# Joining the sign and the low bits of a 64-bit weight: a 16-bit write beside the sign, a shift with one source, and one joining operation

## The chip, the cores and the metric

The kernel runs on one core of a Trainium2 chip. The metric is device time in microseconds (us), lower is better; the runs of the kernel before have a median of 466.94 us. The engines are named as in the profile: PE is TensorE (matrix products), DVE is VectorE, ACT is ScalarE, POOL is GpSimd, SP is the engine that issues most transfers.

## The reference

A block-wise linear attention with decay runs over 2 x 8 heads, 768 positions and 64 dimensions in 12 blocks of 64. Its output, as 1536 tokens of 512 numbers, goes through two layers one after the other.

```python
for b in range(nb):                                   # 12 blocks of 64 positions
    intra = (qb @ kb.T * Dmask) @ vb
    inter = (qb * lam_pow) @ kv_state
    out[:, :, sl] = intra + inter
    kv_state = lam_block * kv_state + (kb * rev_pow).T @ vb
x = out as (1536, 512)
h = x @ moe_w_in;  g = maximum(0.01 * h, h);  x = g @ moe_w_out      # 512 -> 2048 -> 512
h = x @ moe2_w_in; solu = h * softmax(h)                             # 512 -> 1024
ln = (solu - mean) / sqrt(var + 1e-6) * moe2_g_ln
return ln @ moe2_w_out                                               # 1024 -> 512
```

The kernel receives the weight matrices as 64-bit words, read as pairs of 32-bit integers; the second word of a pair has the sign and the high part of the number, the first word the rest of it.

## The kernel before, in words

A weight tile `raww` holds 128 partitions x 2 halves x 512 pairs of words; `raw[:, :, 0]` is the low word, `raw[:, :, 1]` the high word of a pair (stride 8 bytes). Twenty-four tiles come in the list `order`: 16 of kind "io" (one half for `w_in`, one for `w_out`), 4 of kind "a", 4 of kind "b". Each is turned into a 32-bit number `x` by five operations and then split into a high and a low part for products in two terms:

- `words(n)` on ACT: L291 scales the high word, read as float32, into `x`; L292 scales the upper 16 bits of the low word into a small integer.
- `convert(n)` on DVE: L300 clamps `x`; L301 and L302 shift it by three bits and put in sign and low bits.
- `high(n)` on ACT (L322) rounds `x` to the high part in `wio`, `low(n)` on DVE (L340) subtracts to get the low part.

The first two tiles are converted in halves (IN, OUT: 512 columns), the others whole (1024 columns), so L300, L301 and L302 each occur 26 times: 4 times with 512 and 22 times with 1024 columns.

Every engine executes its instructions in the order in which the function writes them; nothing reorders them. The attention steps 0 to 3 are written out by hand at the start, mixed with the conversion of tiles 0 and 1. Step s has scores on PE (L169), their masking on DVE (`scores_ev`, L177), products L201, L210 and L183 on PE, the state update on DVE (L194), and the copies of x to `xhi` (ACT, L256) and `xlo` (DVE, L260); POOL scales with decays (`scale_k` L153, `scale_q` L141, `decay_state` L163). Then a loop runs over 48 items (block of 512 tokens, chunk of w_in): item i does 12 products L350 into one of two banks `hps`; ACT applies the leaky maximum in place (L353) and copies (L356); DVE subtracts (L357); then the high and low part of tile i+1, `convert` of i+2, `words` of i+3; and PE does the 12 products L366 of item i-1. Item 2 also does the scores of step 4 into the other bank, `spare`, between its L350 and its L366; L177 for them is written behind `high` and `low` of tile 3, and item 3's L350 write to that bank. Items 0 to 2 have their `convert` and `words` placed by hand:

```python
        if i == 1:
            words(3)
            convert(3)
            words(4)
        else:
            convert(pair_at(i, 2))
            words(pair_at(i, 3))
```

After the 48 items come twelve token tiles of the second layer (L384, the normalization, transposes L424, L446).

Of the kernel before, what the change touches and what calls it, by code (L numbers as in the profile page):

```python
# [11 lines left out]
U16 = mybir.dt.uint16  # L12
AF = mybir.ActivationFunctionType
ALU = mybir.AluOpType
# [23 lines left out]
LO_SCALE = 7.4375 / 2.0**16  # L38
# [3 lines left out]
def fused_kernel(ctx: ExitStack, tc: tile.TileContext, att, vt, tab, cst, w_in, w_out, w_in2, w_out2, out):  # L42
# [13 lines left out]
    pe, dve, act, pool, sync = nc.tensor, nc.vector, nc.scalar, nc.gpsimd, nc.sync  # L56
# [227 lines left out]
    def words(n, halves=BOTH):  # L284
        if n >= len(order):
            return
        raw = raws[n][:, halves].rearrange("p h a b -> p (h a) b")
        if n not in xs_t:
            xs_t[n] = tmp.tile([P, 2, 512], F32, tag="s", name="x")
        x = xs_t[n][:, halves].rearrange("p h a -> p (h a)")  # L290
        act.activation(x, raw[:, :, 1].bitcast(F32), AF.Copy, scale=HI_SCALE)  # L291
        act.activation(raw[:, :, 0], raw.bitcast(U16)[:, :, 1], AF.Copy, scale=LO_SCALE)  # L292

    def convert(n, halves=BOTH):
        if n >= len(order):
            return
        raw = raws[n][:, halves].rearrange("p h a b -> p (h a) b")
        x = xs_t[n][:, halves].rearrange("p h a -> p (h a)")
        xu = x.bitcast(U32)
        dve.tensor_scalar(x, x, HI_MAX, -HI_MAX, op0=ALU.min, op1=ALU.max)  # L300
        dve.scalar_tensor_tensor(raw[:, :, 0], xu, 3, raw[:, :, 0], op0=ALU.logical_shift_left, op1=ALU.bitwise_or)  # L301
        dve.scalar_tensor_tensor(xu, xu, 0x80000000, raw[:, :, 0], op0=ALU.bitwise_and, op1=ALU.bitwise_or)  # L302

    hi_t = {}

# [183 lines left out]
    x_early(0, xb[0])  # L489
    state_ev(0, kb)  # L490
    words(0, IN)
    x_hi(0, xb[0])
    words(0, OUT)
    convert(0, IN)
    x_lo(0, xb[0])
    decay_state(1, pool)
# [7 lines left out]
    state(1, kb)  # L504
    low(0, IN)
    convert(0, OUT)
    scale_k(2, act)
    x_hi(1, xb[1])
# [13 lines left out]
    scores_ev(3, sb)  # L522
    state_ev(2, kb)
    words(1, IN)
    x_hi(2, xb[0])
    x_lo(2, xb[0])
    convert(1, IN)
    words(1, OUT)
    x_early(3, xb[1])
# [157 lines left out]
```

## Time and profile before

| | |
|---|---|
| median of 3 runs | 466.94 us (466.72, 466.94, 468.98) |
| the profiled execution's own time | 467.06 us |
| its span | 465.3 us (time 1.76 us above the span) |
| mean granted TensorE clock | 0.989 of full speed |
| busy in the span | PE 449.8 us, DVE 262.1, ACT 187.2, POOL 53.3 |

The span runs from the first to the last instruction on the core; times in the views below count from its start. A group of matmuls shows when the first began and how long until the last ended, and the bracket behind a row gives the idle time of that engine before it, with the instruction that ended the wait.

### The profile page before, as it was taken

To read this page: it belongs to the slowest core of one execution; us is meant where nothing else is said; L and a number is where in the kernel's file an instruction comes from. 1 tells how busy PE (TensorE), PEld (TensorE's weight loads), DVE (VectorE), ACT (ScalarE), POOL (GpSimd) and SP (SyncE) were. 2 spreads that over 40 slices of the span, in tenths; PEclk is the share of its full clock that TensorE was granted. 3 is DMA by queue.
4 is the path that set the end of the run, shared out by engine and by line. 5 is a ranking of instruction groups with operands and counts; after the bars stand their busy time and mean duration, and the time that the engine had idled before them with its cause. 6 is when DMAs were issued, how large, how long until landed. Compare 5 with 4: busy or idle time off the path is not lost.

```text
span 465.3 us, 7890 instructions
## 1 busy us (share of the span) xinstructions
PE 449.8 (97%) x3332; PEld 370.8 (80%) x3332; DVE 262.1 (56%) x417; ACT 187.2 (40%) x311; POOL 53.3 (11%) x57
## 2 busy tenths in 40 slices
PE   6788999999999999999999999999999999999997
PEld 3765788888888888888888888888888888888886
DVE  4697899999832121211131888912877666666651
ACT  3657667557332222122244777622322222222221
POOL 2434041240403030100000000000000000000000
PEclk9798999999999999999999999999999999999999
DMA  8999064931302020100015542000000000000001
GB/s 273 337 350 370 4 229 173 323 118 66 92 0 93 1 92 1 46 0 2 1 48 213 191 180 92 0 0 2 0 24 23 24 23 23 24 23 24 23 24 45
DMA packets 16659, 41.61 MB, mean 89 GB/s; under 512 B 1904, under 2 KB 4976, under 8 KB 16112
## 3 DMA queue, kind: packets, MB, share of 16 engines
q1 hardware_dynamic: 16400, 40.71, 24.9%
q8 instruction: 26, 0.43, 0.4%
q10 hardware_dynamic: 224, 0.39, 0.3%
q14 instruction: 9, 0.07, 0.0%
HBM read 37.95 MB, written 3.15 MB: 88 GB/s over the span
## 4 chain that ended last, share of the span: by engine, by line
PE 90%; DMA 3%; DVE 3%; ACT 1%; issue 1%; SPq 0%; ACTq 0%
PE hps L350 28%; PE acc L366 27%; PE acc L446 14%; PE hps L384 7%; PE aps L384 7%; DMA ldw<-in_att_dram 3%; PE acc L424 2%; PE aps L210 2%; PE aps L201 2%; PE hps L169 1%; DVE raww L301 1%; DVE x L302 1%; ACT wio L322 0%; DVE xlo L260 0%; DVE state L194 0%
## 5 line engine op out<-in xcount | busy, mean ns | idle before, releaser
L350 PE MATMUL hps<-xhi,wio 128*128 128x512 f32 x384 | 104.0, 393 | 3.2 <-ACT wio L322 2.2
L357 DVE TENSOR_TENSOR glo<-hps,ghi 128x512 fp32r<-128x512 f32 x48 | 33.2, 691 | 122.5 <-ACT ghi L356 121.2
L366 PE MATMUL acc<-ghi,wio 128*128 128x512 f32 x384 | 96.0, 392 | 0.0
L350 PEld LDWEIGHTS hps<-xhi,wio 128*128 128x128 f32 x384 | 72.3, 189 | 19.2 <-ACT wio L322 2.6
L353 ACT ACTIVATE hps<-hps 128x512 f32<-128x512 f32 x48 | 28.0, 582 | 143.4 <-PE hps L350 143.4
L366 PEld LDWEIGHTS acc<-ghi,wio 128*128 128x128 f32 x384 | 71.4, 188 | 15.1
L350 PE MATMUL hps<-xlo,wio 128*128 128x512 f32 x192 | 52.3, 395 | 1.2 <-DVE xlo L260 1.2
L366 PE MATMUL acc<-glo,wio 128*128 128x512 f32 x192 | 51.3, 389 | 0.0
L446 PE MATMUL acc<-wb,lnhi 128*128 128x512 f32 (+1 forms) x208 | 46.0, 374 | 0.3 <-ACT lnhi L432 0.3
L350 PEld LDWEIGHTS hps<-xlo,wio 128*128 128x128 f32 x192 | 36.5, 191 | 9.4 <-DVE xlo L260 1.7
L446 PEld LDWEIGHTS acc<-wb,lnhi 128*128 128x128 f32 x208 | 36.9, 188 | 7.4 <-ACT lnhi L432 0.6
L366 PEld LDWEIGHTS acc<-glo,wio 128*128 128x128 f32 x192 | 36.1, 188 | 7.5
L416 POOL TENSOR_TENSOR small<-small,nhalf 128x1 f32<-128x1 f32 x12 | 6.6, 548 | 251.7 <-DVE small L415 243.3
L301 DVE SCALAR_TENSOR_TENSOR raww<-x,raww 128x1024 uint32<-128x1024 uint32 (+1 forms) x26 | 32.0, 1231 | 1.2 <-ACT raww L292 0.3
L302 DVE SCALAR_TENSOR_TENSOR x<-x,raww 128x1024 uint32<-128x1024 uint32 (+1 forms) x26 | 31.6, 1214 | 0.9
L291 ACT ACTIVATE x<-raww 128x1024 f32<-128x1024 f32 (+1 forms) x26 | 27.9, 1073 | 2.2 <-DMA raww<-in_w_in_dram 2.2
L356 ACT CAST ghi<-hps 128x512 fp32r<-128x512 f32 x48 | 28.2, 587 | 1.5
L292 ACT ACTIVATE raww<-raww 128x1024 uint32<-128x1024 uint16 (+1 forms) x26 | 28.0, 1077 | 0.0
L141 POOL TENSOR_TENSOR qk<-qk,qpow 128x512 f32<-128x512 f32 x8 | 12.2, 1525 | 122.5 <-PE hps L169 122.5
L384 PE MATMUL hps<-wa,xhi 128*128 128x512 f32 x96 | 24.2, 394 | 0.0
L384 PE MATMUL aps<-wa,xhi 128*128 128x512 f32 x96 | 24.2, 394 | 0.0
L446 PE MATMUL acc<-wb,lnlo 128*128 128x512 f32 (+1 forms) x104 | 24.0, 373 | 0.0
(82 smaller groups left out, 527.1 us busy)
## 6 DMA issues: line engine op xcount, KB each, us to landing
raww<-in_w_out_dram SPq DMA_DIRECT2D x24, 512.0 KB, 6.8
raww<-in_w_in_dram SPq DMA_DIRECT2D x16, 512.0 KB, 6.8
raww<-in_w_in_dram SPq DMA_DIRECT2D x4, 1024.0 KB, 4.8
out_dram<-osb SPq DMA_DIRECT2D x11, 256.0 KB, 2.0
qk<-in_att_dram SPq DMA_DIRECT2D x8, 256.0 KB, 4.2
qk<-in_att_dram SPq DMA_DIRECT2D x16, 128.0 KB, 4.6
kv<-in_att_dram SPq DMA_DIRECT2D x8, 256.0 KB, 3.0
kv<-in_vt_dram SPq DMA_DIRECT2D x8, 256.0 KB, 3.8
```

What stands on the lines that cost most here:

```text
L141: eng.tensor_tensor(qs_t[s], q, qpow, op=ALU.mult)
L291: act.activation(x, raw[:, :, 1].bitcast(F32), AF.Copy, scale=HI_SCALE)
L292: act.activation(raw[:, :, 0], raw.bitcast(U16)[:, :, 1], AF.Copy, scale=LO_SCALE)
L301: dve.scalar_tensor_tensor(raw[:, :, 0], xu, 3, raw[:, :, 0], op0=ALU.logical_shift_left, op1=ALU.bitwise_or)
L302: dve.scalar_tensor_tensor(xu, xu, 0x80000000, raw[:, :, 0], op0=ALU.bitwise_and, op1=ALU.bitwise_or)
L350: pe.matmul(bank, w[:, s, k], x[b][:, k], start=(i == 0), stop=(i == len(terms) - 1))
L353: act.activation(bank, bank, AF.Prelu, alpha=0.01)
L356: act.copy(ghi, bank)
L357: dve.tensor_tensor(glo, bank, ghi.bitcast(F32), op=ALU.subtract)
L366: pe.matmul(acc[m], w[:, s, m], g, start=(f == 0 and first), stop=(f == NF - 1 and last))
L384: pe.matmul(bank, x[b][:, k, o : o + P], w2_t["a", k, half][:, s], start=(i == 0), stop=(i == len(terms) - 1),)
L446: pe.matmul(po[:, 0:n], x[:, k], w2_t["b", k][:, s, cols], start=(i == 0), stop=(i == len(terms) - 1))
```

## The change

L292 writes its small integer (0 to 7) as a 16-bit integer into the lower half of the high word, beside the sign, where it went as a 32-bit integer into the low word. L301 now only shifts `x` in place: one source, one scalar (`tensor_scalar`), where it was an operation with two tensor sources that also joined the low bits. L302 takes sign and low bits with one mask, 0x80000007, from the high word and joins them to the shifted `x`. The number of instructions is the same on every engine.

```diff
-        act.activation(raw[:, :, 0], raw.bitcast(U16)[:, :, 1], AF.Copy, scale=LO_SCALE)
+        act.activation(raw.bitcast(U16)[:, :, 2], raw.bitcast(U16)[:, :, 1], AF.Copy, scale=LO_SCALE)
...
         dve.tensor_scalar(x, x, HI_MAX, -HI_MAX, op0=ALU.min, op1=ALU.max)
-        dve.scalar_tensor_tensor(raw[:, :, 0], xu, 3, raw[:, :, 0], op0=ALU.logical_shift_left, op1=ALU.bitwise_or)
-        dve.scalar_tensor_tensor(xu, xu, 0x80000000, raw[:, :, 0], op0=ALU.bitwise_and, op1=ALU.bitwise_or)
+        dve.tensor_scalar(xu, xu, 3, None, op0=ALU.logical_shift_left)
+        dve.scalar_tensor_tensor(xu, raw[:, :, 1], 0x80000007, xu, op0=ALU.bitwise_and, op1=ALU.bitwise_or)
```

On DVE, the order of instructions stays; two of every three conversion instructions take another form. The piece is the conversion of tile 2, the low part of tile 2 (L340) and the conversion of tile 3, in the first two items; a name in "waits" is the engine or transfer queue whose semaphore the instruction waits for.

```order
 L300 TENSOR_SCALAR x<-x 128x1024
-L301 SCALAR_TENSOR_TENSOR raww<-x,raww 128x1024 [waits DMAHW2_49,DMAHW1_49,DVE_49]
-L302 SCALAR_TENSOR_TENSOR x<-x,raww 128x1024 [waits DVE_49]
+L301 TENSOR_SCALAR x<-x 128x1024 [waits DVE_49]
+L302 SCALAR_TENSOR_TENSOR x<-raww,x 128x1024 [waits DMAHW2_49,DMAHW1_49,DVE_49]
 L357 TENSOR_TENSOR glo<-hps_84,ghi 128x512 [waits Activation_49]
 L340 TENSOR_TENSOR wio<-x,wio 128x1024 [waits Activation_49]
 L300 TENSOR_SCALAR x<-x 128x1024 [waits Activation_49]
-L301 SCALAR_TENSOR_TENSOR raww<-x,raww 128x1024 [waits DMAHW3_49,DMAHW4_49,DVE_49,Activation_49]
-L302 SCALAR_TENSOR_TENSOR x<-x,raww 128x1024 [waits DVE_49]
+L301 TENSOR_SCALAR x<-x 128x1024 [waits DVE_49]
+L302 SCALAR_TENSOR_TENSOR x<-raww,x 128x1024 [waits DMAHW3_49,DMAHW4_49,DVE_49,Activation_49]
```

What moved is the wait for the tile's low bits (Activation, that is L292) from L301 to L302.

On ACT, L292 now writes into words that L291, directly ahead of it on the same engine, reads. The piece is the high part of tile 2, then `words` of tiles 3 and 4, then the first two operations on item 2's bank (L353, L356).

```order
 L322 CAST wio<-x 128x1024 [waits DVE_49]
 L291 ACTIVATE x<-raww 128x1024 [waits DMAHW4_49,DMAHW3_49]
-L292 ACTIVATE raww<-raww 128x1024
+L292 ACTIVATE raww<-raww 128x1024 [waits Activation_49]
 L291 ACTIVATE x<-raww 128x1024 [waits DMAHW6_49,DMAHW5_49]
-L292 ACTIVATE raww<-raww 128x1024
+L292 ACTIVATE raww<-raww 128x1024 [waits Activation_49]
 L353 ACTIVATE hps_83<-hps_83 128x512 [waits PE_49]
 L356 CAST ghi<-hps_83 128x512 [waits Activation_49]
```

Each L292 has gained a wait for ACT's own semaphore, that is for the end of the L291 ahead of it; this holds for all 26.

## Rows read from the trace of the kernel before

**Rows 1.** Busy time of each engine by stretch; then PE clock, DMA share, GB/s.
```profile
24.00:52.00 28.00, 23.27 (x195) 17.64 (x191) 23.92 (x31) 16.68 (x23) 8.64 (x7) 0.94 0.81 290
52.00:440.00 388.00, 387.28 (x2610) 321.61 (x2609) 216.57 (x334) 152.34 (x243) 36.10 (x36) 1.00 0.19 65
```

**Rows 2.** Chain of waits, 24 to 60 us: start, length, what.
```profile
25.98 1.00 DVE raww L301
...
34.71 1.98 DVE raww L301
36.72 1.53 DVE x L302
38.27 1.05 ACT wio L322
...
39.37 4.62 PE hps L350 x12
...
47.75 0.69 DVE r L177
...
48.57 3.00 PE hps L350 x12
```

**Rows 3.** One line's instructions on DVE: count, shortest/median/longest in ns.
```profile
L300 DVE TENSOR_SCALAR x<-x x26: 419/686/1181, 9.8 to 297.5; 128x1024 f32<-128x1024 f32 x22, 128x512 f32<-128x512 f32 x4
L301 DVE SCALAR_TENSOR_TENSOR raww<-x,raww x26: 693/1226/1969, 10.7 to 298.2; 128x1024 uint32<-128x1024 uint32 x22, 128x512 uint32<-128x512 uint32 x4
```

**Rows 4.** Timelines of POOL and DVE: start, length, instruction, [idle before].
```profile
34.22 1.38 POOL L163 TENSOR_TENSOR sd<-state,qpow 128x512 f32<-128x512 f32 x1 [6.78 <-DVE state L194]
35.56 3.16 POOL L153 TENSOR_TENSOR kv<-kv,dmask 128x256 f32<-128x256 f32 x2
45.45 1.29 POOL L141 TENSOR_TENSOR qk<-qk,qpow 128x512 f32<-128x512 f32 x1 [6.73 <-PE hps L169]
46.20 1.63 DVE L340 TENSOR_TENSOR wio<-x,wio 128x1024 fp32r<-128x1024 f32 x1 [0.26 <-ACT wio L322]
...
61.81 1.06 POOL L163 TENSOR_TENSOR sd<-state,qpow 128x512 f32<-128x512 f32 x1
61.65 0.68 DVE L260 TENSOR_TENSOR xlo<-aps,xhi 128x512 fp32r<-128x512 f32 x1
62.24 1.18 DVE L300 TENSOR_SCALAR x<-x 128x1024 f32<-128x1024 f32 x1
```

**Rows 5.** Timeline of PE at the idle gaps and at the scores of step 4.
```profile
20.59 1.15 PE L201 MATMUL acc<-r,ldw 64*64 64x64 f32 x32 [1.72 <-DVE r L177]
28.72 1.21 PE L350 MATMUL hps<-xlo,wio 128*128 128x512 f32 x4 [1.23 <-DVE xlo L260]
...
36.09 1.07 PE L366 MATMUL acc<-glo,wio 128*128 128x512 f32 x4
39.37 1.84 PE L350 MATMUL hps<-xhi,wio 128*128 128x512 f32 x4 [2.21 <-ACT wio L322]
...
43.91 1.46 PE L169 MATMUL hps<-qk 64*64 64x64 f32 x32
```

**Rows 6.** PE alone by quarter microsecond: length, PE busy, PE clock, DMA.
```profile
19.25:19.50 0.25, 0.00 (x0) 1.00 0.86 315
39.75:40.00 0.25, 0.25 (x2) 0.50 1.08 442
```

**Rows 7.** Timeline of ACT in items 0 to 2.
```profile
30.89 0.58 ACT L353 ACTIVATE hps<-hps 128x512 f32<-128x512 f32 x1 [0.15 <-PE hps L350]
31.50 0.59 ACT L356 CAST ghi<-hps 128x512 fp32r<-128x512 f32 x1
...
41.33 1.14 ACT L291 ACTIVATE x<-raww 128x1024 f32<-128x1024 f32 x1
42.36 1.16 ACT L292 ACTIVATE raww<-raww 128x1024 uint32<-128x1024 uint16 x1
44.02 0.58 ACT L353 ACTIVATE hps<-hps 128x512 f32<-128x512 f32 x1 [0.50 <-PE hps L350]
```

## The prediction

> **What bounds the kernel now.** I read the windows by stage first. From 52 to 440 us PE is busy 387.28 of 388 us at full clock while DVE has 216.57 and ACT 152.34 us of work [rows 1]: 18 of the 24 tiles are converted there, or just ahead of it, under matmuls that do not wait, and nothing saved on DVE can shorten that stretch. From 24 to 52 us PE is busy only 23.27 of 28 us and DVE 23.92 [rows 1]. The gain must come from here.
>
> The chain of waits says where: it runs on DVE through L301 at 25.98, and again through L301 and L302 of tile 2 (34.71 to 38.25), then ACT's L322 (38.27), then item 2's L350 (39.37), for which PE sat idle 2.21 us [rows 2, 5]. Later L177 at 47.75 holds back item 3's L350 (48.57); from there on the chain is PE alone [rows 2]. So the change is worth what it moves that one start, 48.57.
>
> The third view is the clock. [...] The gaps of 1.23 us (before 28.72) and 1.72 us (before 20.59) were not followed by a fall; in the latter the clock stood at 1.00 [rows 5, 6].
>
> **What the new forms cost.** The shift has one SBUF source and one scalar, as L300 has: 419 ns for 512 and 686 ns for 1024 columns when nothing hinders it. The old L301 took 693 and 1226 ns [rows 3]. No shift with one source stands in the trace, so I bound it by these rows, and take the lower one: same instruction, tile and element size. Saved: 0.27 us per half tile, 0.54 us per whole tile. L302 reads one dense and one 8-byte-strided tensor, as before; I cost its exchange of operands at nothing. If it were slower, it would show at once, since ACT and then PE wait for L302 at 38.25.
>
> POOL matters, because in the places on the chain it works beside DVE. L300 took 1.18 us at 62.24, where POOL's L163 ran until 62.87: the end, 63.42, is L163's end plus 0.55, as if L300 had only done its first 0.14 us and then waited for POOL. L163, already running, kept its 1.06 us [rows 3, 4]. The old L301 of tile 2 obeys the same: POOL's L163 ended at 35.60, L301 at 36.68, which is 1.08 later, or its 1226 ns less the same 0.14 [rows 2, 4]. L260 with one source in SBUF and one in PSUM overlapped the start of L163 and kept 0.68 us [rows 4]. So both forms of L301 wait out POOL's operation, and only the rest is shortened.
>
> [...]
>
> ACT pays for the new wait. L291 at 41.33 takes 1.14 us but the next instruction starts 1.03 us later, 0.11 us before its end; L353 and L356, with such a wait between them, start 0.61 apart at 0.58 us each, so 0.03 after the end [rows 7]. Each L292 of a whole tile thus starts about 0.14 us later. [...] The duration with a 16-bit output is in no row; I take today's 1.16 us (lower bound: 1.14, L291 with its dense 32-bit output). An upper bound: twice that, 2.3 us; nothing in the trace comes near it.
>
> **The sum, place by place.**
>
> 1. Before 25.98 us nothing on the chain changes: tile 0's halves are converted while DVE and ACT wait for attention inputs, and the first L350 wait for x.
> 2. Tile 1, first half: L301 took 1.00 us with POOL's L153 beside it [rows 2]. It saves 0.27 us. L302, `x_lo` (L260) and PE's L350 at 28.72 follow 0.27 earlier; PE's wait of 1.23 shrinks to 0.96 [rows 5]. ACT's L353 at 30.89 had 0.15 us of idleness before it [rows 7]; L292 of tile 2, ahead of it, comes 0.27 earlier and pays 0.14, so L353 still follows PE. Everything to L300 of tile 2 shifts by 0.27.
> 3. Tile 2: L163 and L301 both shift by 0.27; behind L163's end the shift needs 0.55 us where L301 needed 1.08. L302 behaves as before (POOL's L153 goes first, then it). L302 ends 0.27 + 0.54 = 0.81, say 0.80 us earlier, L322 starts at 37.47, item 2's L350 at 38.57. PE's preceding work, which ended at 37.16 [rows 5], ends at 36.89; the gap becomes 1.68 us.
> 4. The clock: 1.68 is below 1.72, after which it did not fall, and well below 2.21. I take it that it stays at full speed. Twelve L350 take 3.00 us and end at 41.57 instead of 43.98.
> 5. Now ACT is late: L353 stood behind L292 of tile 4, which would have let it start at 42.36 + 1.05 = 43.41 (1.05 is the step from one to the next in these rows), 0.6 before it did [rows 7]. After the change: 43.41 − 0.80 + 2 x 0.14 = 42.89, against 44.02. So 1.13 us earlier, and PE's 1.6 us from the clock are partly lost in this queue.
> 6. DVE's L340 follows ACT's L322 of tile 3 and starts at 45.07. Before it took 1.63 us, since POOL's L141 ran to 46.74 [rows 4]; L141 follows the scores (1.46 us [rows 5]), which now end at 43.0, so it is over by 44.4. L340 then takes 1.23 us like the other operation with two SBUF sources [rows 3]: 0.40 us more. L177 at 47.75 − 1.13 − 0.41 = 46.21, and item 3's L350 0.82 us behind it, as before: 47.03.
>
> 48.57 − 47.03 = 1.54 us. The work behind it shifts whole: PE is full, ACT's 0.14 us per item and DVE's saved 0.54 lie under it. The remaining 21 or so conversions save some 11 us of DVE's time that nobody waits for. The profiled execution took 467.06 us, 0.12 above the median of the runs shown; its sum is 465.52, and from the median 466.94 it is **465.4 us**, 0.33% faster. What a measurement tells from no change is about 0.5%, 2.3 us, so this counts as "same".
>
> **Rivals.**
>
> - *The clock falls again at 38.6 to 39.6* (chance 0.2). For it: 1.68 lies between a gap with and a gap without a fall, and the 1.72 one had other work ahead of it. Then twelve L350 still take 4.62 us, ACT's queue costs nothing (0.50 us idle [rows 7] against 0.28), L340 meets POOL again, and only step 3's shift stays: 0.80 us, 466.1.
> [...]
> - *The change does nothing here* (0.08). The shift stays at 1226 ns and waits for POOL as well. The waits on ACT hide in 0.50 and 0.15 us of idleness: 466.9.
> - *Slower: ACT becomes the bound* (0.05). The place is step 5: L353 stands behind two L292. If 16-bit writes at a stride of 8 bytes made each 1.16 us longer, L353 would start at 42.89 + 2.3 = 45.2, L177 near 48.5, PE at 49.3 after 3.3 us of idleness, and a clock at 0.50 would add 1.6: 2.4 us lost, 469.3. It decides from about 0.75 us more per L292, where the 1.54 is used up. Nothing in the profile speaks for such a price: L291 and L292 differ by 0.02 us with a dense or a strided output [rows 7].
>
> The forecast has 0.5 (its own range 465.0 to 465.8); 0.07 is left for what I have not seen. **The range** reaches from the 1x rival to no change, 464.7 to 466.9; left out are the slow rival, part of the unseen and the edges. Faster than 464.6 needs more than any case gives: 0.06. Slower than 469.3: 0.03. Within: 0.91.
>
> **What the profile of the changed kernel would show.** L301 as TENSOR_SCALAR with 0.42 and 0.69 us at the least, longer beside POOL (right), or a median near 1.2 (wrong). L292 starting 0.03 after L291's end, still 1.16 long. PE's gap before item 2 near 1.7, and a PE clock of 1.00 behind it; L353 of item 2 waiting for no engine but following L292; L340 at 1.23; a gap of about 1 us on PE before item 3, as L177's r comes last. From there PE must be full to the end; the prediction is wrong if the clock falls in another place, if an L292 is much longer, or if PE starts item 3 later than about 48.

## The result: slower, through the price of the 16-bit write

The changed kernel takes 470.46 us (median of 9 runs, 468.67 to 473.11) against 466.94 us (9 runs): ratio 1.0078, 95% interval 1.0051 to 1.0104. The interval lies wholly above 1, so the kernel is slower, by 0.8%. The forecast was 465.4 us. The profiled execution of the changed kernel is the longest of its nine, 473.11 us with a span of 471.3 us. Single executions of some kernels below ran longer as a whole by tens of microseconds or far more; medians, ratios and the profiles that are read leave them out.

Its lines for the three changed instructions, in the view that [rows 3] come from (count, shortest/median/longest in ns):

```profile
L292 ACT ACTIVATE raww<-raww x26: 1342/2564/2620, 9.4 to 298.6; 128x1024 uint16<-128x1024 uint16 x22, 128x512 uint16<-128x512 uint16 x4
L301 DVE TENSOR_SCALAR x<-x x26: 427/694/1436, 10.2 to 305.0; 128x1024 uint32<-128x1024 uint32 x22, 128x512 uint32<-128x512 uint32 x4
L302 DVE SCALAR_TENSOR_TENSOR x<-raww,x x26: 691/1226/1531, 10.8 to 305.7; 128x1024 uint32<-128x1024 uint32 x22, 128x512 uint32<-128x512 uint32 x4
```

L301 fell from 1226 to 694 ns as forecast and L302 did not change. L292, which took 1.15 us, takes 2.56 us. On ACT (timeline of items 0 to 2, the counterpart of [rows 7]):

```profile
31.33 2.53 ACT L292 ACTIVATE raww<-raww 128x1024 uint16<-128x1024 uint16 x1
33.60 0.74 ACT L353 ACTIVATE hps<-hps 128x512 f32<-128x512 f32 x1
...
40.61 1.04 ACT L322 CAST wio<-x 128x1024 fp32r<-128x1024 f32 x1 [3.37 <-DVE x L302]
...
42.73 2.51 ACT L292 ACTIVATE raww<-raww 128x1024 uint16<-128x1024 uint16 x1
44.99 1.17 ACT L291 ACTIVATE x<-raww 128x1024 f32<-128x1024 f32 x1
46.20 2.51 ACT L292 ACTIVATE raww<-raww 128x1024 uint16<-128x1024 uint16 x1
48.45 0.75 ACT L353 ACTIVATE hps<-hps 128x512 f32<-128x512 f32 x1
```

L353 of items 0 and 2 now both start without an idle bracket, directly behind L292. The order on the engine holds them back, not a semaphore: PE had ended their products at 32.43 and 46.05 us, 1.17 and 2.40 us earlier, and no wait in the view names it. From L322 of tile 2 to item 2's L353 it is 7.84 us; before it was 44.02 − 38.27 = 5.75 [rows 2, 7]. DVE and PE (timelines, to compare with [rows 4, 5]):

```profile
37.59 1.44 DVE L301 TENSOR_SCALAR x<-x 128x1024 uint32<-128x1024 uint32 x1
50.79 1.22 DVE L340 TENSOR_TENSOR wio<-x,wio 128x1024 fp32r<-128x1024 f32 x1 [0.26 <-ACT wio L322]
```

```profile
28.33 1.20 PE L350 MATMUL hps<-xhi,wio 128*128 128x512 f32 x4 [0.72 <-ACT xhi L256]
41.71 1.20 PE L350 MATMUL hps<-xhi,wio 128*128 128x512 f32 x4 [2.99 <-ACT wio L322]
52.77 1.55 PE L350 MATMUL hps<-xhi,wio 128*128 128x512 f32 x4 [2.15 <-DVE r L177]
54.11 1.91 PE L350 MATMUL hps<-xlo,wio 128*128 128x512 f32 x4
```

A stretch that can be compared between kernels is the one from item 0's first L350 to item 3's first. Here it is 52.77 − 28.33 = 24.44 us; before, in the profile of [rows 2], 48.57 − 26.29 = 22.28 us (item 0 began there at 26.29). It splits at the two L353 and at L322: L353 of item 0 comes 0.67 us later after item 0's first product (5.27 against 4.60), from there to L322 it takes 0.37 less (7.01 against 7.38: the saving of the shift, less an L353 that takes 0.74 in place of 0.58), to item 2's L353 2.09 more, and from there to item 3's L350 0.23 less (4.32 against 4.55, mainly L340 at 1.22 in place of 1.63). Sum: +2.16 us. The first 0.67 hides a part that varies without the change: the second group of item 0's products starts 1.98 us after the first here, 2.43 before, and 2.01 in a kernel below whose first three tiles are those of before. Behind item 3's start the granted clock fell to 0.50 (1.91 us for four products in place of 1.07) and its twelve took 4.57 us, 1.57 more than before.

The remaining difference of the two spans, 6.0 us, is 0.24 us in the items with conversions (below) and 2.04 us ahead of 28.33, which the change does not explain: item 0 began between 26.35 and 28.80 us in the profiles of the kernels below, at 28.70 in the one whose first three tiles are those of before. The clock differs there: from 24 to 26 us it stood at 0.50 in the changed kernel and in that one, and at 1.00 before.

### The profile page after: what moved, and what is told of

It is laid out like the page before. It is cut to its first block, busy times and chain, and to the rows that moved or that the text cites. A ratio compares the mean times of both kernels' runs of the same rounds, so it can differ in the third digit from the quotient of the medians.

```text
span 471.3 us, 7892 instructions
## 1 busy us (share of the span) xinstructions
PE 452.9 (96%) x3332; PEld 372.8 (79%) x3332; DVE 248.9 (53%) x417; ACT 221.0 (47%) x311; POOL 51.9 (11%) x57
## 4 chain that ended last, share of the span: by engine, by line
PE 88%; DMA 9%; ACT 1%; issue 0%; DVE 0%; SPq 0%; ACTq 0%
PE acc L366 27%; PE hps L350 26%; PE acc L446 14%; PE hps L384 7%; PE aps L384 7%; DMA ldw<-in_vt_dram 3%; PE acc L424 2%; DMA raww<-in_w_in_dram 2%; PE aps L210 2%; DMA raww<-in_w_out_dram 2%; PE aps L201 2%; DMA qk<-in_att_dram 1%; DMA ldw<-in_att_dram 1%; PE hps L169 1%; ACT raww L292 1%
## 5 line engine op out<-in xcount | busy, mean ns | idle before, releaser
L350 PE MATMUL hps<-xhi,wio 128*128 128x512 f32 x384 | 105.0, 396 | 5.9 <-ACT wio L322 3.0
L357 DVE TENSOR_TENSOR glo<-hps,ghi 128x512 fp32r<-128x512 f32 x48 | 33.2, 692 | 141.0 <-ACT ghi L356 141.0
L350 PEld LDWEIGHTS hps<-xhi,wio 128*128 128x128 f32 x384 | 72.7, 191 | 22.5 <-ACT wio L322 4.1
L353 ACT ACTIVATE hps<-hps 128x512 f32<-128x512 f32 x48 | 30.9, 643 | 118.7 <-PE hps L350 118.7
L292 ACT ACTIVATE raww<-raww 128x1024 uint16<-128x1024 uint16 (+1 forms) x26 | 61.9, 2381 | 0.9
L350 PE MATMUL hps<-xlo,wio 128*128 128x512 f32 x192 | 52.8, 398 | 0.8 <-DVE xlo L260 0.8
L350 PEld LDWEIGHTS hps<-xlo,wio 128*128 128x128 f32 x192 | 36.7, 192 | 9.0 <-DVE xlo L260 1.2
L302 DVE SCALAR_TENSOR_TENSOR x<-raww,x 128x1024 uint32<-128x1024 uint32 (+1 forms) x26 | 31.5, 1213 | 1.9 <-ACT raww L292 1.0
L356 ACT CAST ghi<-hps 128x512 fp32r<-128x512 f32 x48 | 28.2, 587 | 1.5
L291 ACT ACTIVATE x<-raww 128x1024 f32<-128x1024 f32 (+1 forms) x26 | 28.0, 1075 | 1.6 <-DMA raww<-in_w_in_dram 1.6
L141 POOL TENSOR_TENSOR qk<-qk,qpow 128x512 f32<-128x512 f32 x8 | 13.7, 1708 | 126.9 <-PE hps L169 126.9
L404 ACT ACTIVATE e<-hps,small 128x512 f32<-128x512 f32 x12 | 8.2, 686 | 35.8 <-DVE small L402 35.8
```

The costliest lines, as they stand in the source:

```text
L141: eng.tensor_tensor(qs_t[s], q, qpow, op=ALU.mult)
L292: act.activation(raw.bitcast(U16)[:, :, 2], raw.bitcast(U16)[:, :, 1], AF.Copy, scale=LO_SCALE)
L302: dve.scalar_tensor_tensor(xu, raw[:, :, 1], 0x80000007, xu, op0=ALU.bitwise_and, op1=ALU.bitwise_or)
L350: pe.matmul(bank, w[:, s, k], x[b][:, k], start=(i == 0), stop=(i == len(terms) - 1))
L353: act.activation(bank, bank, AF.Prelu, alpha=0.01)
L356: act.copy(ghi, bank)
```

## Experiments

Theory W: the strided 16-bit write is slow, and what it costs is decided by ACT's queue ahead of L353. Rival D: the new forms on DVE cost the time. Rival A: the added wait of ACT for itself does. Later rival S: each dear write costs time wherever it stands. Medians of the kernel before on the same chips were 467.5 to 467.7 us; each ratio is taken against the runs of its own chip.

**The shift with a 32-bit write (sign left out)**

```diff
+        act.activation(raw[:, :, 0], raw.bitcast(U16)[:, :, 1], AF.Copy, scale=LO_SCALE)
         dve.tensor_scalar(xu, xu, 3, None, op0=ALU.logical_shift_left)
+        dve.scalar_tensor_tensor(xu, raw[:, :, 0], 0x7, xu, op0=ALU.bitwise_and, op1=ALU.bitwise_or)
```

> The shift with one source is kept, L292 writes 32 bits into the low word again and L302 takes the low bits from there; the sign is left out, so that no third tensor is needed. Theory W (the 16-bit write is what costs): L292 back at 1.15 us, no wait for L291, L301 at 0.69 us, and the time falls below that of the kernel before, as the sum on record had it: 465 to 466 us, ratio to the kernel before 0.996 to 0.999. Rival D (the new forms on DVE, through POOL or the chain, cost the time): about 470 us, ratio 1.007. Rival A (the added wait of ACT for itself costs it): below 467 too, since that wait is gone here.

Measured: 466.12 us, ratio 0.9972 (0.9956 to 0.9988). This is the kernel whose time the prediction had worked out, but for the self-wait. Its timelines:

```profile
35.75 1.43 DVE L301 TENSOR_SCALAR x<-x 128x1024 uint32<-128x1024 uint32 x1
46.08 1.22 DVE L340 TENSOR_TENSOR wio<-x,wio 128x1024 fp32r<-128x1024 f32 x1 [0.25 <-ACT wio L322]
```

```profile
42.87 1.13 ACT L292 ACTIVATE raww<-raww 128x1024 uint32<-128x1024 uint16 x1
43.91 0.57 ACT L353 ACTIVATE hps<-hps 128x512 f32<-128x512 f32 x1
```

```profile
39.87 1.19 PE L350 MATMUL hps<-xhi,wio 128*128 128x512 f32 x4 [1.65 <-ACT wio L322]
48.05 1.17 PE L350 MATMUL hps<-xhi,wio 128*128 128x512 f32 x4 [0.84 <-DVE r L177]
```

L301 beside POOL took 1.43 us (the sum on record: 34.44 to 35.88, 1.44), the gap before item 2 was 1.65 (1.68), the clock stayed up (granted 1.00 from 35 to 60 us), L353 followed L292 without idleness, L340 met no POOL (L141 ended at 45.66 us, before it started), and 0.84 us of idleness (about 1) came before item 3. The stretch from item 0 to item 3 is 20.28 us, 2.00 less than in the profile before; the part on the second price list says why this is not all the shift's. Rival D falls: with the new forms on DVE alone the kernel is faster.

**The write with two-source operations**

```diff
+        act.activation(raw.bitcast(U16)[:, :, 2], raw.bitcast(U16)[:, :, 1], AF.Copy, scale=LO_SCALE)
+        dve.scalar_tensor_tensor(raw[:, :, 0], xu, 3, raw[:, :, 1], op0=ALU.logical_shift_left, op1=ALU.bitwise_xor)
+        dve.scalar_tensor_tensor(xu, raw[:, :, 1], 0x7FFFFFF8, raw[:, :, 0], op0=ALU.bitwise_and, op1=ALU.bitwise_xor)
```

> The 16-bit write beside the sign is kept; L301 and L302 both have two tensor sources, as before the change (x shifted and joined by exclusive or with the whole high word, then the unwanted bits of the high word taken out by exclusive or). Theory W: L292 at 2.5 us for 1024 columns, L301 at 1.23 us, and the time is at or above that of the changed kernel, 470 to 472 us, ratio to the kernel before 1.007 to 1.011. Rival D: about 467 us. Rival A: about 470 us, as the wait is here too, with L292 itself at 1.15 us.

Measured: 474.08 us, ratio 1.0139 (1.0112 to 1.0165), more than expected. L292 has a median of 2578 ns. The stretch from item 0 to item 3 is 24.92 us, 2.64 more than before. From the end of item 3's twelve L350 to the end of the span it takes 1.41 us longer than before, where the changed kernel takes 0.24 longer. In the items with conversions ACT does not keep up either, as its timeline in a late one shows:

```profile
76.81 0.82 ACT L353 ACTIVATE hps<-hps 128x512 f32<-128x512 f32 x1
...
80.33 2.59 ACT L292 ACTIVATE raww<-raww 128x1024 uint16<-128x1024 uint16 x1
82.61 0.79 ACT L353 ACTIVATE hps<-hps 128x512 f32<-128x512 f32 x1
```

From L353 to L353 it is 5.80 us, and PE's item is 2 x 2.72 = 5.44 us. ACT falls behind by 0.36 us per item, until an attention step gives PE more to do and ACT catches up (its L353 at 90.76 waits 1.60 us for PE). The changed kernel is hardly better: its L353 at 76.79 and 82.56 are 5.77 us apart. With the old forms ACT's L322 at 92.27, behind that attention step, also waits 0.30 us for DVE's L302; its counterpart in the changed kernel, at 91.81, waits for nothing.

**The self-wait with a 32-bit write**

```diff
-        act.activation(raw[:, :, 0], raw.bitcast(U16)[:, :, 1], AF.Copy, scale=LO_SCALE)
+        act.activation(raw[:, :, 1], raw.bitcast(U16)[:, :, 1], AF.Copy, scale=LO_SCALE)
```

with `raw[:, :, 1]` for `raw[:, :, 0]` in L301 and L302 as well.

> The kernel before, with one difference: L292 writes its 32 bits into the high word, which L291 has read, and L301 and L302 take the low bits from there (the sign comes from x, as before). So L292 waits for L291 as in the changed kernel, with a 32-bit write. Theory W: L292 at 1.15 us, starting 0.03 us after L291's end, the time within 0.1% of the kernel before: 466.7 to 467.3 us. Rival A: 469 us or more. Rival D: as theory W.

Measured: 467.98 us, ratio 1.0014 (0.9997 to 1.0031): not to be told from no change. The wait is there and has its price, on ACT's timeline:

```profile
39.06 1.15 ACT L291 ACTIVATE x<-raww 128x1024 f32<-128x1024 f32 x1
40.24 1.17 ACT L292 ACTIVATE raww<-raww 128x1024 uint32<-128x1024 uint16 x1
```

L292 starts 1.18 us after L291, where it was 1.03 [rows 7]: 0.15 us (0.14 was forecast), with L292 itself at 1.17. Rival A, which wanted 469 us or more, falls as the cause of the loss; the interval leaves the wait 0.31% at most.

**What exactly is dear: two lists of prices.** Single operations were put where the engines wait in the second layer of the kernel before, on tiles that nothing else uses, in this manner:

```diff
+            act.activation(d32[:, :, 0], s16[:, :, 1], AF.Copy, scale=0.5)
+            act.activation(d16[:, :, 2], s16[:, :, 1], AF.Copy, scale=0.5)
...
+            act.activation(d16p[:, 0:512, 0], s16[:, :, 1], AF.Copy, scale=0.5)
```

> The kernel before, with single operations of 128x512 added in the second layer, where ACT, DVE and POOL wait; they read and write tiles that nothing else uses. They vary one thing at a time: 16 or 32 bits written, packed or at a stride of 4 or 8 bytes, from a strided 16-bit or a packed 32-bit input, on ACT, DVE and POOL. Theory W1 (16-bit elements that do not fill a 4-byte word cost more than one step on ACT): about 0.68 us for 32-bit outputs at any stride and for packed 16-bit ones, 1.34 us for 16-bit ones at a stride of 4 or 8 bytes, in either half of the word and from either input. Rival W2 (any 16-bit output on ACT is slow): 1.34 us for packed ones as well. Rival W3 (it is reading and writing the same words in place): 0.68 us in this list for all, since input and output are different tiles.

Groups by line and form, 512 elements per partition (busy us, mean ns; the line tells which pattern):

```profile
L622 ACT ACTIVATE pdst<-psrc 128x512 uint16<-128x512 uint16 x1 | 1.4, 1396 | 0.0
L631 ACT ACTIVATE pdst<-psrc 128x512 bf16<-128x512 f32 x1 | 1.4, 1390 | 0.0
L620 ACT ACTIVATE pdst<-psrc 128x512 uint16<-128x512 uint16 x1 | 1.4, 1369 | 0.0
L629 ACT ACTIVATE pdst<-psrc 128x512 uint16<-128x512 f32 x1 | 1.4, 1367 | 0.0
L625 ACT ACTIVATE pdst<-psrc 128x512 uint16<-128x512 uint16 x1 | 0.8, 807 | 0.0
L619 ACT ACTIVATE pdst<-psrc 128x512 uint32<-128x512 uint16 x1 | 0.7, 690 | 0.0
L628 ACT ACTIVATE pdst<-psrc 128x512 uint16<-128x512 f32 x1 | 0.7, 652 | 0.0
...
L635 DVE TENSOR_SCALAR pdst<-psrc 128x512 uint16<-128x512 uint16 x1 | 0.7, 744 | 0.0
L634 DVE TENSOR_SCALAR pdst<-psrc 128x512 uint32<-128x512 uint16 x1 | 0.4, 416 | 0.0
```

All four of 1.37 to 1.40 us write 16 bits at a stride of 8 bytes: into the lower half of the first (L622) or the second word (L620), as bf16 (L631), from a packed 32-bit input (L629). At a stride of 4 bytes (L625) it is 0.81, packed (L628) 0.65, and 32 bits at 8 bytes (L619) 0.69. So neither the 16-bit type by itself (W2) nor writing in place (W3) is the cause; it is 16 bits at a stride. W1 holds at 8 bytes and misses at 4, where the stride costs only 0.12 to 0.15 us. DVE loses too: 0.74 (L635) against 0.42 us (L634).

The second list has the same manner with other patterns.

> Single operations of 128x256 (and 128x128) on ACT from a packed 32-bit input, and of 128x512 on DVE, placed as in the first list. Written are 32 bits at a stride of 8 and 16 bytes, 16 bits packed and at a stride of 4, 8, 16 and 32 bytes. If it is a narrow write at a stride of 8 bytes or more that costs, 16 bits take about 1.04 ns more per element than 32 bits at 8 bytes and the same or more at 16 and 32; if it is the step from one 16-byte group to the next, 32 bits at a stride of 16 bytes are dear as well. On DVE 16 bits at 4 bytes should then lie between the packed 0.42 and the 0.74 us of a stride of 8.

Its instructions, from the view of the written tile (shortest/median/longest in ns):

```profile
L620 ACT ACTIVATE pdst<-psrc x1: 458/458/458, 335.9 to 335.9; 128x256 uint32<-128x256 f32 x1
L621 ACT ACTIVATE pdst<-psrc x1: 662/662/662, 336.4 to 336.4; 128x256 uint32<-128x256 f32 x1
L623 ACT ACTIVATE pdst<-psrc x1: 532/532/532, 345.2 to 345.2; 128x256 uint16<-128x256 f32 x1
L624 ACT ACTIVATE pdst<-psrc x1: 781/781/781, 345.8 to 345.8; 128x256 uint16<-128x256 f32 x1
L626 ACT ACTIVATE pdst<-psrc x1: 1380/1380/1380, 355.9 to 355.9; 128x256 uint16<-128x256 f32 x1
L627 ACT ACTIVATE pdst<-psrc x1: 418/418/418, 357.3 to 357.3; 128x256 uint16<-128x256 f32 x1
L629 ACT ACTIVATE pdst<-psrc x1: 790/790/790, 367.7 to 367.7; 128x128 uint16<-128x128 f32 x1
L630 ACT ACTIVATE pdst<-psrc x1: 310/310/310, 368.5 to 368.5; 128x128 uint16<-128x128 f32 x1
L632 DVE TENSOR_SCALAR pdst<-psrc x1: 459/459/459, 380.9 to 380.9; 128x512 uint16<-128x512 f32 x1
```

In order: 32 bits at 8 and 16 bytes; 16 bits at 4, 8, 16 bytes and packed; then, with 128 elements, at 32 bytes and packed; last DVE at 4 bytes, between the packed 0.43 and 0.75 at 8. Both halves of the expectation hold in part: 32 bits at 16 bytes cost 0.80 ns more per element than at 8 ((662 − 458) / 256), and 16 bits at 16 bytes about twice those at 8 per element. The section on the hardware draws the numbers together.

Up to the second layer both lists run the kernel before, so their profiles show its first items twice more. PE in the first list, then in the second:

```profile
40.03 1.75 PE L350 MATMUL hps<-xhi,wio 128*128 128x512 f32 x4 [2.19 <-ACT wio L322]
```

```profile
39.42 1.19 PE L350 MATMUL hps<-xhi,wio 128*128 128x512 f32 x4 [2.23 <-ACT wio L322]
...
47.60 1.16 PE L350 MATMUL hps<-xhi,wio 128*128 128x512 f32 x4 [0.83 <-DVE r L177]
```

In the first list the clock fell to 0.50 behind the gap, item 2's twelve products took 4.61 us, and the stretch from item 0 to item 3 is 22.28 us, as in the profile of [rows 2]. In the second it stood at 1.00 behind an equal gap, the twelve took 3.02 us, and the stretch is 20.94 us, 1.34 less. The fall is thus not a fixed part of the kernel before. Against this execution without a fall the shift alone (20.28) gains 0.66 us in the stretch, and the changed kernel (24.44) loses 3.50.

**Where the loss arises.** The forms were chosen by tile: `if n >= 5` (then `n in (3, 4)`, then `n == 2`) takes the changed lines, every other tile those of before.

> The changed forms for tiles 5 to 23, the forms of before for tiles 0 to 4. Theory W with the loss in the first items (ACT's queue is late only where PE waits for it): L292 at 2.5 us for 19 tiles, yet no difference to the kernel before that can be told, ratio 0.998 to 1.002. Rival S (each of the dear writes costs time wherever it stands): about 3 us slower, ratio 1.006.

Measured: 467.24 us, ratio 1.0000 (0.9984 to 1.0017), with 19 writes at a median of 2577 ns. Rival S falls.

> The changed forms for tiles 3 and 4 alone, whose L292 stand ahead of item 2's L353 on ACT. Theory W: each L292 2.5 us and 0.12 us later, so L353 about 2.1 us later than in the kernel before, L177 and PE's item 3 about 1.8 us later, with PE idle for some 2 us ahead of item 3; 1.8 us slower if the clock stays up there, up to 3.4 us if it falls: ratio 1.004 to 1.007. Rival S: 2 of 24 tiles, 0.3 us, ratio 1.001.

Measured: 472.30 us, ratio 1.0092 (1.0070 to 1.0114), above the expected 1.004 to 1.007: two tiles lose as much as all 24 (the two intervals overlap). A further run of the same kernel gives its profile.

> The kernel with the changed forms for tiles 3 and 4 alone once more, for a profile of it. Theory W: item 2's L353 directly behind the second dear L292, about 2.1 us later than in the kernel before, PE idle for 2 us or more ahead of item 3, and the granted clock at 0.50 behind that gap as well as behind the one before item 2, which would explain 4 us in place of 1.8.

Measured: 470.91 us. ACT and PE (here L293 is the 16-bit write, L357 the products L350 and L360 is L353):

```profile
45.85 2.54 ACT L293 ACTIVATE raww<-raww 128x1024 uint16<-128x1024 uint16 x1
48.13 0.73 ACT L360 ACTIVATE hps<-hps 128x512 f32<-128x512 f32 x1
```

```profile
41.34 1.20 PE L357 MATMUL hps<-xhi,wio 128*128 128x512 f32 x4 [2.19 <-ACT wio L329]
52.44 1.16 PE L357 MATMUL hps<-xhi,wio 128*128 128x512 f32 x4 [3.75 <-DVE r L177]
```

From item 2's first product to its L353 it is 6.79 us, before 4.65: 2.14 more (2.1 expected). To item 3's first product it is 11.10, before 9.20: 1.90 more (1.8 expected). The other half of the expectation missed: the clock did not fall behind either gap (granted 1.00 from 41 to 60 us). From item 0's first product (28.70) to item 3's it is 23.74 us, 1.46 more than in the profile before, which had a fall, and 2.80 more than in the second price list, which had none. The timed runs of this kernel had a mean granted clock of 0.977 to 0.985, this one 0.989; that falls of the clock make up the rest of the 0.92% is likely from that, but no profile shows it.

> The changed forms for tile 2 alone, whose L292 stands ahead of item 0's L353. Theory W: L353 1.1 us later, from there L357 and L300 of tile 2; the shift gives back 0.54 us, so item 2's first product about 0.55 us later: ratio 1.000 to 1.003. If the chain did not run through ACT there, the shift alone would count, 0.5 us faster and no fall of the clock: ratio 0.997.

Measured: 468.44 us, ratio 1.0009 (0.9993 to 1.0024), within the expected range but not to be told from no change. Item 0's L353 stands directly behind the dear write:

```profile
31.75 2.55 ACT L293 ACTIVATE raww<-raww 128x1024 uint16<-128x1024 uint16 x1
34.04 0.76 ACT L360 ACTIVATE hps<-hps 128x512 f32<-128x512 f32 x1
```

The clock did not fall behind its gap of 2.99 us before item 2. Counted from item 0's, item 2's first product comes 0.60 us later than in the execution of the kernel before without a fall (0.55 expected) and item 3's 0.61 later; against the profile of [rows 2], which had a fall, item 3's comes 0.73 us earlier.

**The changed kernel with `words(4)` behind item 2's L353**

```diff
             words(3)
             convert(3)
-            words(4)
         else:
+            if i == 2:
+                words(4)
             convert(pair_at(i, 2))
```

> The changed kernel with the same move: only one of the dear L292 stands ahead of item 2's L353. Theory W with the place in ACT's queue: L353 follows PE's products instead of L292, about 2.4 us earlier, and 1.5 to 2.5 us of the loss come back: 468 to 469 us, ratio 1.002 to 1.005. Rival S (the cost of a dear write does not depend on its place): no difference to the changed kernel, ratio 1.008.

Measured: 469.92 us, ratio 1.0045 (1.0025 to 1.0064): the ratio is within what theory W expects, the time 0.9 us above. The changed kernel has 1.0078, and the two intervals overlap, so this run by itself does not show that the move gains. No profile of it is read.

**A version with a cheap write: sign first.** L292 writes 32 bits as before; one two-source operation joins sign and low bits in the low word before `x` is needed, for tile 2 ahead of item 0's L357, where DVE was idle (0.96 us in the profile before); after the clamp one operation shifts and joins.

```diff
+        dve.scalar_tensor_tensor(
+            raw[:, :, 0], raw[:, :, 1], 0x80000000, raw[:, :, 0], op0=ALU.bitwise_and, op1=ALU.bitwise_or
+        )
...
         dve.tensor_scalar(x, x, HI_MAX, -HI_MAX, op0=ALU.min, op1=ALU.max)
+        dve.scalar_tensor_tensor(xu, xu, 3, raw[:, :, 0], op0=ALU.logical_shift_left, op1=ALU.bitwise_or)
...
     words(2)
+    join(2)
     l1_split((0, 0), hps[0])
```

> A version of its own with the 32-bit write: one two-source operation joins sign and low bits in the low word before x is needed, and after the clamp one two-source operation shifts x and joins it; for tile 2 the first of these stands ahead of L357 of item 0, where DVE sat idle. The number of operations is that of the kernel before. If PE's start in the first items follows DVE's chain, L302's successor for tile 2 ends about 1.57 us earlier, PE's gap before item 2 shrinks from 2.2 to about 0.65 us, the clock stays up, and then ACT's queue limits: item 3 starts about 2.5 us earlier, 464.3 us (463.8 to 465.5), ratio 0.994 to 0.997. Rival: another wait or a fall of the clock gives it back, 466 to 467.5 us.

Measured: 465.51 us, ratio 0.9963 (0.9944 to 0.9982). DVE and PE (here L298 is the join, L314 the shift, L362 the products):

```profile
31.24 1.22 DVE L298 SCALAR_TENSOR_TENSOR raww<-raww 128x1024 uint32<-128x1024 uint32 x1
34.97 1.97 DVE L314 SCALAR_TENSOR_TENSOR x<-x,raww 128x1024 uint32<-128x1024 uint32 x1
```

```profile
38.07 1.21 PE L362 MATMUL hps<-xhi,wio 128*128 128x512 f32 x4 [0.66 <-ACT wio L334]
46.31 1.16 PE L362 MATMUL hps<-xhi,wio 128*128 128x512 f32 x4 [0.86 <-DVE r L177]
```

The gap before item 2 is 0.66 us (0.65 expected). With item 0's start at 26.57 the stretch is 19.74 us, 2.54 less than in the profile before (2.5 expected) and 1.20 less than in its execution without a fall; the ratio stands for 1.7 us.

> The version that joins sign and low bits first, with one more move: words of tile 4 are written behind item 2's L353, L356 and L322 in place of ahead of them. If ACT's queue ahead of L353 is the limit there (it follows the last L292 without idleness in that version), L353 comes about 1 us earlier, as soon as PE is done, PE's gap before item 3 goes, and the time falls by a further 0.8 us: 464.5 to 465, ratio to the kernel before 0.993 to 0.996. Rival: the two words of item 3 together (4.2 us) make the next L353 late and give it back: ratio 0.996 to 0.999.

Measured: 465.03 us, ratio 0.9941 (0.9920 to 0.9963), not to be told from the version without the move. The expected end of PE's gap before item 3 missed: it stayed at 0.86 us. Counted from item 0's start L353 came 1.12 us earlier, but ACT's high part of tile 3 (here L334) then waited for DVE's conversion of that tile (here L314), which had itself waited 0.85 us for the tile's L292:

```profile
43.11 1.05 ACT L334 CAST wio<-x 128x1024 fp32r<-128x1024 f32 x1 [0.89 <-DVE x L314]
```

Both versions beat the kernel before and the changed one.

## Why the prediction was wrong

**The step that failed** is the price of L292: "The duration with a 16-bit output is in no row; I take today's 1.16 us", with "twice that, 2.3 us" as the upper bound. It measured 2.56 us, above even that bound, and 1.34 to 1.36 for 512 columns. All the rows of ACT that it went by write 32 bits, so none could speak of a narrower write, and "nothing in the trace comes near it" was taken for evidence. The slow rival named the place and mechanism, L353 behind two L292, and had a chance of 0.05; its condition, about 0.75 us more per L292, was exceeded at 1.4 us. Against the forecast of 465.4 the median is 5.1 us later. The range stopped at no change, although this bound lay outside it. The chances do not close either: 0.91 within, 0.06 faster and 0.03 "Slower than 469.3" add up to 1 and leave nothing for 466.9 to 469.3, where the slow rival's own 469.3 lies.

**The bound and the place** were right: every tile from the sixth on is converted under PE's matmuls (the text says 18 of 24 tiles; they are 19), and dear writes there cost nothing that could be measured (ratio 1.0000). They are not quite free: "ACT's 0.14 us per item" became some 1.5 us, ACT's item passed PE's 5.44 us (5.77, and 5.80 with the old forms on DVE), and in the changed kernel's chain one in three groups of twelve L350 there takes 2.80 us and not 2.72: 0.24 us in all.

**The forms on DVE** (0.42 and 0.69 us, waiting out POOL) were right to 0.01 us, L302 at no cost too. Tile 2's shift ended 0.55 us behind POOL's L163, both in the changed kernel (39.03 against 38.48 us) and with the shift alone (37.18 against 36.63). No run shows the 1x rival that the range names for its lower end, 464.7 us, a shift that does not wait for POOL. **The self-wait** was right (0.15 against 0.14 us), and hidden.

**The sum for what was left** was right in size: without the dear write, 1.3 us gained (0.9972 of 467.5) where 1.54 was forecast. Each wait of the stretch was where the sum had it, but the agreement of the totals is in part luck, as the next paragraph shows.

**The clock**: the sum took the fall to 0.50 in its one profile [rows 6], where item 2's twelve products took 4.62 us and item 3's 3.00 [rows 2], for a part of the kernel before, and step 4 took the length of a gap as the sign. In the profile of the second price list the kernel before has the same gap and no fall, and against that execution the shift gains 0.66 us and not 1.54, all of it at item 2's first product (12.10 against 12.76 us after item 0's). The row given for the gap of 1.72 us lies inside that gap; behind it, from 20.5 to 28 us, the clock stood at 1.00 too. The gap of 1.65 us was indeed without a fall, but so were 2.19 and 3.75 us in the one profile for tiles 3 and 4 and 2.99 us with tile 2 alone, while 2.19 with the self-wait (1.91 us for four products), 2.21 before and, 1.4 us into the products, 2.99 in the changed kernel had one. The length of the idle gap alone does not tell. Since ACT limits item 2's L353 in the changed kernel (2.40 us behind the end of PE's products), the fall behind item 2's start there cost nothing; the one behind item 3 cost 1.57 us in the profiled execution. How much of the 3.5 us in the medians is from such falls stays open.

## What to carry to other kernels

Before a write is made narrower to save another operation, time that write with its own width and stride: here 0.53 us saved per tile on DVE cost 1.4 us per tile on ACT, whose queue stood ahead of what PE waited for. Where a row for a form is missing, twice the price of another form is no bound, and the range must hold what the path does with a price beyond it. To find who waits for a longer instruction, read the order on its engine: here L353, which stands behind it, came 2.09 us later, and no wait in the trace named it. Before a stall is put into a sum as something to be won back, look whether other executions of the same kernel have it.

## What the runs showed of the hardware

In the two lists a 16-bit write at a stride on ACT took, per element, 1.07 ns at 4 bytes ((807 − 532) / 256, one row from either list) and 2.29 ns at 8 bytes ((1367 − 781) / 256). For 16 and 32 bytes there is one size each, so these are estimates, worked out with the fixed part of the packed write, which takes 0.84 ns per element ((418 − 310) / 128): 0.84 + (1380 − 418) / 256 = 4.6 ns at 16 bytes and 0.84 + (790 − 310) / 128 = 4.6 at 32. So the price doubled from 4 to 8 and from 8 to 16 bytes and was the same at 32; counted by the 16-byte pieces of the tile that receive something, it is 4.3 to 4.6 ns per piece, whether four, two or one 16-bit elements go into it. With 32-bit elements it is far less: 0.91 ns per element at 8 bytes ((690 − 458) / 256, one row from either list), and at 16 bytes 0.80 ns more. Why, no run here shows.
